# Weight blocks seven to fifteen of a three-layer kernel: ScalarE's first steps wait for the attention rows of chunks zero and one

## The chip, the cores and the metric

One NeuronCore of a Trainium2 chip runs the whole program. The metric is the device time of one execution in microseconds, the median of three runs. Each profile is one execution, taken by the hardware profiler.

## What is computed

Three layers follow one another on 3072 tokens (4 sequences of 768 positions) of width 384.

```
# layer 1: linear attention with the delta rule, one 48 x 48 state per batch and head, 8 heads
y[t]  = q[t] @ state
state = state + beta[t] * outer(k_n[t], v[t] - k_n[t] @ state)     # t = 0 .. 767
# layer 2: x = y as (3072, 384);  384 -> 2048 -> 384
h = x @ w_in
x = (h * sigmoid(1.702 * h)) @ w_out
# layer 3: four experts, 384 -> 1024 -> 384, all of them on every token
out = sum over e of  p[:, e] * (relu(x @ w1[e]) @ w2[e])           # p: normed domain_probs
```

The weights of layer 2 arrive as 64-bit floats; everything else is 32-bit.

## The kernel before

**Attention.** The 768 positions are cut into 12 chunks of 64 positions. Chunk u of all 4 sequences gives 256 rows for layer 2, and two chunks make a tile of 512 rows; there are six tiles. A chunk is a chain that mostly alternates between TensorE and the engines that read its result: keys against the state (L867), a subtraction on VectorE (L874), a first solve (L881), copies to SBUF on ScalarE and VectorE (L184, tile `su`), a cross term (L896), L874 again, a second solve (L881), copies again, the output y (L912 and L913, in two halves), and the state update (L936, added by L953 on VectorE). The inverse that the solves use is made per tile. For tile 0 VectorE makes it. For all later tiles VectorE transposes the Gram matrix (L637), computes norms and rates in small operations (L399 to L425), and GpSimd then runs a chain of 30 elimination steps (L649, then L658 and L660 in turn, then L665); VectorE transposes the result back (L685). The chain of a chunk can't start before that.

**Rows for layer 2.** Chunks 0 and 1 write their rows straight into the operand of layer 2: `take_x` on ScalarE or VectorE (L184, tile `xs`) takes the rounded part, `take_rest` (L930) on VectorE the rest. These tasks are `direct[0]` and `direct[1]`. Later chunks copy y into `stage`, move a fourth of it by DMA (L1049), and are split into `xs` from there (L184 and L1083).

**Layer 2 and its weights.** The weights are 16 blocks f. For each block, layer1 (L1089) makes 128 hidden rows from `xs`, the gate (L1211 and L1213 on ScalarE, L1214 on VectorE) makes `gh`, and layer2_1 (L1196) adds the result into `px`. Each is nine matmuls. Tiles 0 and 1 are halved: blocks 0 to 7 run on the first chunk's 256 columns, then on the second chunk's, and only blocks 8 to 15 on all 512 columns. A block's weights are prepared once. `queue_w1` loads it by SyncE (L222, into `rw`, or into `raw` for blocks 0 and 15), converts the 64-bit floats by two steps on ScalarE (`small` at L293, `low` at L296) and one on VectorE (`shift`, L300), and splits it into two 32-bit parts (`hi`, L305 on ScalarE, and `lo`, L308 on VectorE, which ends as `wdone[f]`). There are six `rw` buffers, so the load of block f waits for `wdone[f - 6]`.

**Layer 3** runs after all tiles of layer 2, in L1089, L1323 and L1353.

**What sets the order.** Nothing is reordered on the chip: each engine runs its queue in order. The queues are written by a planner inside the kernel (`Order` and `Task`, L28 to L148). Every step is a task with an engine, an estimated cost, the tasks it depends on and a priority (lower first). The planner keeps a virtual clock per engine and issues the best task that is ready. Between two matmuls of layer 2 it looks again (`tick`), so attention matmuls are woven into layer 2's. When layer 2 needs something that isn't done yet, `until` issues other tasks until it is. A dependency in the task list orders the plan; the waits on the chip come from the data. A step with another dependency therefore moves on its engine, and by the virtual clocks what stands behind it on all engines can move as well.

Weight steps have priorities of 6 (blocks 0 and 1), 16 (2 to 7) and 33 (8 to 15); chunks 0 and 1 have 0 to 10, and `take_x` has -2. An engine that is free takes what is ready, whatever its priority.

Of the kernel before, what the change touches and what calls it, by code (L numbers as in the profile page):

```python
# [27 lines left out]
class Order:  # L28
# [14 lines left out]
    def task(self, fn, eng, cost, deps=(), lat=0.15, prio=0, slack=0.5, can=None, extra=0.4):  # L43
        t = Task(self, fn, eng, cost, [d for d in deps if d is not None], lat, prio, slack, can, extra)
        return t
# [106 lines left out]
def delta_attention_moe_moe_kernel(  # L152
# [27 lines left out]
    task, tick, until = od.task, od.tick, od.until  # L180
# [40 lines left out]
    def bulk(dst, src):  # L221
        nc.sync.dma_start(out=dst, in_=src)  # L222
# [31 lines left out]
    W, wdone, begun, turns, ended, marks = {}, {}, {}, {}, {}, []  # L254
# [3 lines left out]
    def queue_w1(f, after):  # L258

        kw = dict(prio=(FIRST_W if f < 2 else EARLY_W if f < N_EARLY else LATE_W) + f / 50, slack=0.5)
        later = {F1 - 1: (wdone.get(0),)}
        cell = {}

        def room():
            cell["raw"] = wp.tile([128, 1536], F32, name="rw", tag=f"w{RAW + (f - 1) % 6}")  # L270

        def touch():
            room()
            V.memset(cell["raw"][:, 0:1], 0.0)

        def load():
            if f in (0, F1 - 1):
                t = raw.rearrange("p h c -> p (h c)")
            else:
                if "raw" not in cell:  # L280
                    room()
                t = cell["raw"]
            dst = t.bitcast(I32) if wide else t
            bulk(dst if wide else dst[:, 0:768], w[f])
            if wide:
                pairs = dst.rearrange("p (n t) -> p n t", t=2)
                cell["lo"], cell["hi"] = pairs[:, :, 0], pairs[:, :, 1]
                cell["t"], cell["top"] = cell["lo"].bitcast(F32), cell["hi"].bitcast(F32)
            else:
                cell["t"] = t[:, 0:768]  # L290

        def small():
            nc.scalar.activation(out=cell["top"], in_=cell["top"], func=AF.Prelu, scale=2.0 ** -112, alpha=-2.0 ** 32)  # L293

        def low():
            nc.scalar.activation(out=cell["lo"].bitcast(U32), in_=cell["lo"].bitcast(U32), func=AF.Copy, scale=2.0 ** -29 * (1 - 2.0 ** -16),  # L296
                                 bias=7.5 * 2.0 ** -16 - 0.5)

        def shift():
            nc.vector.scalar_tensor_tensor(out=cell["lo"], in0=cell["hi"], scalar=3, in1=cell["lo"],  # L300
                                           op0=ALU.logical_shift_left, op1=ALU.bitwise_or)

        def hi():
            W[f] = wp.tile([128, 2, 768], F32R, name="w", tag=f"w{RING[f]}")
            nc.scalar.copy(out=W[f][:, 0, :], in_=cell["t"])  # L305

        def lo():
            nc.vector.tensor_tensor(out=W[f][:, 1, :], in0=cell["t"], in1=W[f][:, 0, :].bitcast(F32), op=ALU.subtract)  # L308

        if 6 < f < F1 - 1:  # L310
            after = (*after, wdone[f - 6])
        if 1 < f < 7:
            after = (*after, task(touch, "DVE", 0.07, (marks[f - 2],), prio=1.4))
        dep = task(load, "HW", 2.0 if wide else 1.0, (*later.get(f, ()), *after), lat=1.5, prio=50)
        if wide:
            a = task(small, "ACT", 0.83, (dep,), **kw)
            b = task(low, "ACT", 0.9, (dep, begun[0]), **kw)
            dep = task(shift, "DVE", 0.88, (a, b), **kw)
        h = task(hi, "ACT", 0.73, (dep, wdone.get(f - 1)), **kw)
        wdone[f] = task(lo, "DVE", 0.95, (h,), **kw)  # L320
# [47 lines left out]
    direct = {}  # L368
# [725 lines left out]
    with tc.manual_schedule():  # L1094
# [44 lines left out]
        for f in range(F1):  # L1139
            queue_w1(f, placed[3])  # L1140
# [326 lines left out]
```

## Time and profile before

| | us |
|---|---|
| median of three runs | 1367.26 (1365.63 to 1661.65) |
| the profiled execution | 1365.22 |
| its span, first to last instruction | 1363.3 |
| TensorE busy in the span | 1332.3 |
| VectorE, ScalarE, GpSimd busy | 612.2, 423.1, 221.3 |

The span is the part of the execution that the rows below can explain; 1.9 us lie around it. A busy TensorE is one that had a matmul in flight: a wait that falls between two matmuls that overlap is not seen as idle.

### The profile page before, as it was taken

How to read it: one execution, taken by the hardware profiler on the slowest of the kernel's cores; microseconds unless marked ns; L12 is line 12 of the kernel's file. 1: busy time of each engine (PE TensorE's matmuls, PEld its weight loads, DVE VectorE, ACT ScalarE, POOL GpSimd, SP SyncE). 2: the span in 40 equal slices, each digit the busy share in tenths (PEclk: the TensorE clock that was granted, in tenths of full speed). 3: DMA queues.
4: the chain of work that ended last, by engine and by line, in shares of the span. 5: the costliest groups of instructions: out<-in, count | busy, mean ns of one | idle time of the engine just before them, and what ended most of it. 6: DMA issues, size and time to landing. Idle time of an engine off the chain costs nothing.

```text
span 1363.3 us, 28151 instructions
## 1 busy us (share of the span) xinstructions
PE 1332.3 (98%) x12376; PEld 1118.1 (82%) x12376; DVE 612.2 (45%) x1049; ACT 423.1 (31%) x790; POOL 221.3 (16%) x408
## 2 busy tenths in 40 slices
PE   5899999999999999999999999999999999999998
PEld 4788898778787888788888888888888888888888
DVE  7888584663735224223333234433343333233443
ACT  6873442432424334312222122222222221112111
POOL 4295748055181000000000000000000000000000
PEclk9999999999999999999999999999999999999999
DMA  7640412220201013000010000010010000011111
GB/s 238 217 132 14 113 29 76 63 64 2 74 17 40 5 76 124 8 9 31 31 42 20 1 20 31 32 38 14 0 31 31 32 20 8 0 31 31 32 31 47
DMA packets 36411, 63.30 MB, mean 46 GB/s; under 512 B 18688, under 2 KB 20160, under 8 KB 36288
## 3 DMA queue, kind: packets, MB, share of 16 engines
q1 hardware_dynamic: 36288, 61.50, 14.9%
q8 instruction: 97, 1.59, 0.5%
q14 instruction: 26, 0.21, 0.1%
HBM read 52.58 MB, written 7.91 MB: 44 GB/s over the span
## 4 chain that ended last, share of the span: by engine, by line
PE 92%; DVE 4%; DMA 1%; ACT 1%; issue 1%; SPq 0%; DVEq 0%; ACTq 0%
PE ph L1089 43%; PE po L1323 24%; PE px L1196 14%; PE po L1353 5%; PE y L913 2%; PE ch L881 1%; PE ch L867 1%; PE gp L491 1%; PE ch L896 1%; PE ch L936 1%; DMA rw<-in_w_dram 1%; DVE scr L581 1%; PE gp L554 1%; DVE scr L685 0%; DVE scr L184 0%
## 5 line engine op out<-in xcount | busy, mean ns | idle before, releaser
L1089 PE MATMUL ph<-xs,w 128*128 128x512 f32 (+1 forms) x2736 | 651.3, 380 | 1.7 <-ACT x L184 0.8
L1089 PEld LDWEIGHTS ph<-xs,w 128*128 128x128 f32 x2736 | 494.2, 188 | 96.8 <-ACT x L184 1.2
L1384 DVE SCALAR_TENSOR_TENSOR hh<-ph,hh 128x512 fp32r<-128x512 f32 x192 | 132.5, 690 | 503.4 <-ACT hh L1383 503.4
L1323 PE MATMUL po<-hh,w 128*128 128x512 f32 x1440 | 352.4, 389 | 0.0
L1323 PEld LDWEIGHTS po<-hh,w 128*128 128x128 f32 x1440 | 270.4, 188 | 56.0
L1383 ACT ACTIVATE hh<-ph 128x512 fp32r<-128x512 f32 x192 | 114.8, 598 | 616.7 <-PE ph L1089 616.7
L1196 PE MATMUL px<-gh,w 128*128 128x512 f32 (+1 forms) x1008 | 228.7, 364 | 1.0 <-DVE gh L1214 0.8
L1196 PEld LDWEIGHTS px<-gh,w 128*128 128x128 f32 x1008 | 170.7, 188 | 31.6 <-DVE gh L1214 2.1
L1214 DVE TENSOR_TENSOR gh<-ph,gh 128x512 fp32r<-128x512 f32 (+1 forms) x112 | 68.7, 613 | 149.2 <-ACT gh L1213 148.0
L1211 ACT ACTIVATE ph<-ph 128x512 f32<-128x512 f32 (+1 forms) x112 | 58.4, 521 | 176.0 <-PE ph L1089 164.7
L660 POOL TENSOR_TENSOR scr<-scr,itmp 128x30 f32<-128x30 f32 (+9 forms) x150 | 83.9, 559 | 11.8
L658 POOL TENSOR_TENSOR itmp<-scr 128x30 f32<-128x30 f32 (+9 forms) x150 | 79.5, 530 | 11.2
L1353 PE MATMUL po<-w,hh 128*128 128x384 f32 x384 | 73.9, 342 | 0.0
L1353 PEld LDWEIGHTS po<-w,hh 128*128 128x128 f32 x384 | 69.3, 188 | 2.4
L1213 ACT CAST gh<-ph 128x512 fp32r<-128x512 f32 (+1 forms) x112 | 58.8, 525 | 3.5
L184 ACT COPY su<-ch 64x384 f32<-64x384 f32 (+2 forms) x59 | 27.2, 462 | 63.2 <-PE ch L881 62.5
L1183 DVE TENSOR_TENSOR xs<-x,xs 128x512 fp32r<-128x512 f32 x72 | 45.3, 684 | 0.0
L1182 ACT CAST xs<-x 128x512 fp32r<-128x512 f32 x72 | 39.7, 619 | 0.0
L496 DVE TENSOR_TENSOR pq<-gp,pmask 64x512 f32<-64x512 f32 x48 | 33.1, 689 | 7.0 <-PE gp L491 6.1
L250 DVE TENSOR_TENSOR w<-raw,w 128x768 fp32r<-128x768 f32 x32 | 30.7, 958 | 10.2 <-ACT w L249 9.4
L184 DVE COPY su<-ch 64x384 f32<-64x384 f32 (+2 forms) x45 | 24.2, 537 | 21.3 <-PE ch L881 20.4
L953 DVE TENSOR_TENSOR su<-su,ch 48x384 f32<-48x384 f32 x44 | 24.3, 552 | 20.5 <-PE ch L936 10.3
(133 smaller groups left out, 740.8 us busy)
## 6 DMA issues: line engine op xcount, KB each, us to landing
raw<-in_we_dram SPq DMA_DIRECT2D x32, 384.0 KB, 2.9
rw<-in_w_dram SPq DMA_DIRECT2D x14, 768.0 KB, 4.6
raw<-prd SPq DMA_DIRECT2D x20, 256.0 KB, 3.1
k<-in_k_dram SPq DMA_DIRECT2D x12, 384.0 KB, 4.8
kt<-in_kt_dram SPq DMA_DIRECT2D x24, 192.0 KB, 5.0
pq<-in_q_dram SPq DMA_DIRECT2D x24, 192.0 KB, 3.5
v<-in_v_dram SPq DMA_DIRECT2D x12, 384.0 KB, 3.2
out_dram<-oacc SPq DMA_DIRECT2D x80, 48.0 KB, 1.7
```

Source lines behind the costliest of these rows:

```text
L184: (nc.scalar.copy if e == "ACT" else nc.vector.tensor_copy)(out=out_, in_=in_)
L658: E.tensor_tensor(out=tv, in0=x[:, j:j + 1, j + 1:].broadcast_to([128, m, r]), in1=x[:, 0:m, j:j + 1].broadcast_to([128, m, r]), op=ALU.mult)
L660: E.tensor_tensor(out=x[:, 0:m, j + 1:], in0=x[:, 0:m, j + 1:], in1=tv, op=ALU.add)
L1089: mm(ps, lhsT=w[:, a, kk * 128:(kk + 1) * 128], rhs=xs[kk][:, b, cs], start=kk == 0 and i == 0, stop=kk == KD - 1 and i == 2)
L1196: mm(px[d][:, cs], lhsT=w[:, a, 384 + d * 128:384 + (d + 1) * 128], rhs=gh[:, b, 0:cs.stop - cs.start], start=f == 0 and i == 0 and cs.sta ...
L1211: a = task(lambda: nc.scalar.activation(out=ph, in_=ph, func=AF.Gelu_apprx_sigmoid), "ACT", 0.05 + 0.43 * c, (pe,), **kw)
L1213: a = task(lambda: nc.scalar.copy(out=hi, in_=ph), "ACT", 0.05 + 0.43 * c, (a,), **kw)
L1214: a = task(lambda: nc.vector.tensor_tensor(out=lo, in0=ph, in1=hi.bitcast(F32), op=ALU.subtract), "DVE", 0.07 + 0.53 * c, (a,), **kw)
L1323: mm(po[kk], lhsT=w[:, a, 384 + kk * 128:384 + (kk + 1) * 128], rhs=hh[:, c, :], start=f == 0 and i == 0, stop=f == F2 - 1 and i == 2)
L1353: mm(ps, lhsT=hh[:, a, b * 128:(b + 1) * 128], rhs=w[:, c, 384:768].rearrange("p (k a i) -> p a k i", a=4, k=KD), start=f == 0 and i == 0, ...
L1383: nc.scalar.activation(out=hh[:, 0, :], in_=ph, func=AF.Relu)
L1384: nc.vector.scalar_tensor_tensor(out=hh[:, 1, :], in0=ph, scalar=0.0, in1=hh[:, 0, :].bitcast(F32), op0=ALU.max, op1=ALU.subtract)
```

## The change

`small` of blocks 7 and later depends on `direct[0]` too; for blocks 10 to 15, `small` and `low` both depend on `direct[1]` as well. Nothing that is computed changes. One line is added, so every line behind L316 has a number that is higher by one in the changed kernel.

```
         if wide:
-            a = task(small, "ACT", 0.83, (dep,), **kw)
-            b = task(low, "ACT", 0.9, (dep, begun[0]), **kw)
+            rows = direct[1] if f >= 10 else ()
+            a = task(small, "ACT", 0.83, (dep, *rows, *(direct[0] if f >= 7 else ())), **kw)
+            b = task(low, "ACT", 0.9, (dep, begun[0], *rows), **kw)
             dep = task(shift, "DVE", 0.88, (a, b), **kw)
```

The plan is written anew from there. Three places show it.

The first is ScalarE's queue while chunk 0 gives its rows. `raw_69` holds block 15 here; `rw_337`, `rw_525` and `rw_880` (`rw_881` in the change) hold blocks 2, 3 and 7; `y_849` and `y_890` (`y_888`) are the two halves of chunk 0's output. Before:

```order
L184 COPY stage_73<-su_80 128x12x16
L293 ACTIVATE raw_69<-raw_69 128x768
L305 CAST w_882<-rw_337 128x768
L296 ACTIVATE raw_69<-raw_69 128x768
L184 CAST xs_100<-y_849 128x128
L184 CAST xs_101<-y_849 128x128
L184 CAST xs_102<-y_849 128x128
L305 CAST w_920<-rw_525 128x768
L293 ACTIVATE rw_880<-rw_880 128x768
L184 CAST xs_100<-y_890 128x128
L184 CAST xs_101<-y_890 128x128
L184 CAST xs_102<-y_890 128x128
```

And now:

```order
L184 COPY stage_73<-su_80 128x12x16
L305 CAST w_879<-rw_337 128x768
L184 CAST xs_100<-y_849 128x128
L184 CAST xs_101<-y_849 128x128
L184 CAST xs_102<-y_849 128x128
L296 ACTIVATE rw_881<-rw_881 128x768
L184 CAST xs_100<-y_888 128x128
L184 CAST xs_101<-y_888 128x128
L184 CAST xs_102<-y_888 128x128
L305 CAST w_944<-rw_525 128x768
L184 COPY su_80<-ch0_719 48x8x48
L293 ACTIVATE rw_881<-rw_881 128x768
```

Both steps of block 15 and the first step of block 7 have gone from ahead of the rows; block 7's second step (L296), which waits for the same load, stands ahead of the second half of the rows in their place.

The second place is VectorE's queue from the first gate of layer 2 (`gh`) to the transpose with which the inverse of tile 1 begins (L637, L638 in the change). Before:

```order
L300 SCALAR_TENSOR_TENSOR rw<-rw 128x768
L308 TENSOR_TENSOR w<-rw,w 128x768
L1214 TENSOR_TENSOR gh<-ph,gh 128x256 x2
L637 STREAM_TRANSPOSE scr_98<-scr_97 128x1024
L399 TENSOR_SCALAR sm<-scr_98 128x32
```

And now, the last twelve rows up to the transpose:

```order
L1215 TENSOR_TENSOR gh<-ph,gh 128x256
L184 COPY su<-ch_739 48x8x48
L1215 TENSOR_TENSOR gh<-ph,gh 128x256
L308 TENSOR_TENSOR w<-rw,w 128x768
L300 SCALAR_TENSOR_TENSOR rw<-rw 128x768
L1215 TENSOR_TENSOR gh<-ph,gh 128x256
L308 TENSOR_TENSOR w<-rw,w 128x768
L1215 TENSOR_TENSOR gh<-ph,gh 128x256
L300 SCALAR_TENSOR_TENSOR rw<-rw 128x768
L308 TENSOR_TENSOR w<-rw,w 128x768
L1215 TENSOR_TENSOR gh<-ph,gh 128x256
L638 STREAM_TRANSPOSE scr_98<-scr_97 128x1024
```

The transpose stood behind the gates of blocks 0 and 1; it stands behind those of blocks 0 to 4 now.

The third place is ScalarE's queue at the end of tile 0, where chunk 3's chain runs (`ch_2487` before, `ch_2553` now are a bank of it) and tile 1's operand is split from `stage`. Before:

```order
L1211 ACTIVATE ph<-ph 128x512
L1213 CAST gh<-ph 128x512
L184 COPY su<-ch_2487 64x8x48 x2
L1211 ACTIVATE ph<-ph 128x512
L1213 CAST gh<-ph 128x512
L184 COPY su<-ch_2487 64x8x48 x2
L184 CAST xs<-stage 128x256 x2
L1211 ACTIVATE ph<-ph 128x512
L1213 CAST gh<-ph 128x512
L184 COPY stage<-y 48x2x256 x2
L1211 ACTIVATE ph<-ph 128x256
```

And now:

```order
L1212 ACTIVATE ph<-ph 128x512
L1214 CAST gh<-ph 128x512
L184 COPY su<-ch_2553 64x8x48 x4
L184 CAST xs<-stage 128x256 x2
L184 COPY stage<-y 48x2x256 x2
L1212 ACTIVATE ph<-ph 128x256
```

Three gates of 512-column blocks lay within and around chunk 3's chain; one does now, ahead of both copies, so chunk 3's steps follow each other with little of layer 2 between them.

## Rows read from the trace of the kernel before

**Rows 1.** Busy time of each engine by stretch: start:end, length, then the engines.
```profile
0.00:52.60 52.60, 30.03 (x1144) 27.10 (x1144) 43.60 (x100) 36.02 (x70) 16.83 (x38) 1.00 0.72 231
52.60:120.80 68.20, 66.45 (x1261) 60.05 (x1261) 59.10 (x105) 47.08 (x93) 49.66 (x70) 1.00 0.38 116
120.80:155.50 34.70, 34.70 (x827) 27.24 (x827) 21.21 (x52) 13.53 (x28) 18.98 (x39) 1.00 0.23 63
155.50:1357.70 1202.20, 1199.53 (x9138) 1002.41 (x9137) 486.08 (x790) 326.52 (x600) 135.80 (x262) 1.00 0.11 33
```
**Rows 2.** ScalarE in order of time: start, us, instruction, [idle before and releaser].
```profile
46.95 0.95 ACT L293 ACTIVATE raw<-raw 128x768 f32<-128x768 f32 x1 [0.57 <-DMA raw<-in_w_dram]
...
49.40 0.61 ACT L184 CAST xs<-y 128x128 fp32r<-128x128 f32 x3
...
51.49 0.93 ACT L293 ACTIVATE rw<-rw 128x768 f32<-128x768 f32 x1 [0.69 <-DMA rw<-in_w_dram]
52.30 0.61 ACT L184 CAST xs<-y 128x128 fp32r<-128x128 f32 x3
```
**Rows 3.** SyncE's issues in order of time, the loads of blocks 7 to 9.
```profile
47.15 6.26 SPq L222 DMA_DIRECT2D rw<-in_w_dram  x3
```
**Rows 4.** TensorE in order of time: chunk 0's end, then chunks 2 and 3.
```profile
50.37 1.64 PE L936 MATMUL ch<-su,k 64*48 64x48 f32 x64
52.62 0.38 PE L1089 MATMUL ph<-xs,w 128*128 128x256 f32 x1 [0.61 <-ACT xs L184]
...
55.53 1.39 PE L769 MATMUL gp<-scr,scr 32*32 32x16 f32 x128
...
120.82 1.15 PE L867 MATMUL ch<-su,kt 48*64 48x48 f32 x64
...
136.46 1.10 PE L913 MATMUL y<-pq,su 128*48 128x64 f32 x32
...
143.10 0.88 PE L881 MATMUL ch<-v,scr 32*32 32x48 f32 x64
...
155.53 1.24 PE L1089 MATMUL ph<-xs,w 128*128 128x256 f32 x9
```
**Rows 5.** The chain that ended last, in order of time: one 512-column block's layer 1.
```profile
112.71 2.07 PE ph L1089 x9
```
**Rows 6.** VectorE in order of time: tile 1's inverse, two weight shifts, chunk 3's steps.
```profile
57.68 2.18 DVE L637 STREAM_TRANSPOSE scr<-scr 128x1024 f32<-128x1024 f32 x1
...
91.79 2.76 DVE L300 SCALAR_TENSOR_TENSOR rw<-rw 128x768 int32<-128x768 int32 x2
...
118.70 2.22 DVE L685 STREAM_TRANSPOSE scr<-scr 128x1024 f32<-128x1024 f32 x1 [0.49 <-POOL scr L665]
...
140.80 1.70 DVE L874 TENSOR_TENSOR v<-v,ch 128x384 f32<-128x384 f32 x3
...
144.08 1.14 DVE L184 COPY su<-ch 64x384 f32<-64x384 f32 x2 [1.58 <-PE ch L881]
...
151.20 1.22 DVE L1083 TENSOR_TENSOR xs<-stage,xs 128x256 fp32r<-128x256 f32 x3
```
**Rows 7.** GpSimd in order of time: tile 1's elimination chain.
```profile
64.17 4.27 POOL L649 TENSOR_TENSOR scr<-scr,bt 128x256 f32<-128x256 f32 x4 [11.94 <-DVE bt L425]
...
90.44 0.62 POOL L658 TENSOR_TENSOR itmp<-scr 128x240 f32<-128x240 f32 x1
91.13 1.30 POOL L660 TENSOR_TENSOR scr<-scr,itmp 128x240 f32<-128x240 f32 x1
...
116.32 2.34 POOL L665 TENSOR_TENSOR scr<-scr,bt 128x256 f32<-128x256 f32 x4
```
**Rows 8.** L913 alone in two stretches: length, TensorE, its loads, granted clock, DMA.
```profile
45.00:50.30 5.30, 4.98 (x48) 4.35 (x48) 1.00 0.84 292
78.60:80.20 1.60, 1.42 (x24) 1.34 (x24) 1.00 0.75 273
```
**Rows 9.** SyncE in order of time: chunk 2's rows moved within `stage`.
```profile
139.34 4.73 SPq L1049 DMA_DIRECT2D stage<-scr  x6
```

## The prediction

> **What bounds the kernel now.** I read busy time by stretch first. Up to 52.6 us TensorE is busy for 30.0 us; from there to 1357.7 us it waits for 1.75 us in the first stretch, not at all in the second and for 2.67 us in the long third [rows 1]. So the time is the moment at which layer 2 starts, plus a TensorE queue that hardly waits. The matmuls are the same in the changed kernel. It can gain only before 52.6 us or out of those 1.75 and 2.67 us, and it loses whatever wait it makes.
>
> Next I read the queues in order of time. ScalarE stands at 46.95 us for block 15's load. The first half of chunk 0's rows is cast at 49.40. The second half is cast at 52.30, although its y matmuls ended at 50.37 when L936 began: block 7's first step, at 51.49, stood ahead of it and waited for its load [rows 2, 4]. TensorE's first L1089 then begins at 52.62, after 0.61 us of waiting for those casts [rows 4].
>
> Further on, two waits are hidden with little to spare. Tile 1's inverse begins with L637 at 57.68 us, GpSimd gets its input at 64.17 and ends at 118.66, and L685 ends at 120.92; the first matmul of chunk 2, L867, stands in TensorE's queue at 120.82 [rows 4, 6, 7]. TensorE and the inverse arrive together. Chunk 2's last y, at 136.46, ends at 137.56, its rows are moved in `stage` from 139.34 and split by 152.42, and tile 1's first block begins at 155.53 [rows 4, 6, 9]. Three us are left there.
>
> **The change, part by part.** *First rows.* The change takes away from ahead of them block 15's 0.57 us of waiting and two steps of 0.95 us or so, and block 7's first step (0.93 us after 0.69 us of waiting) [rows 2]. The first half of the rows could be cast some 1.5 us earlier. But block 7's second step isn't tied to chunk 0's rows. The plan puts it ahead of the second half, and it needs the same load, issued at 47.15 behind `wdone[1]`, which nothing here makes earlier; the load was there at 51.49 [rows 2, 3]. So that step runs from 51.49 and the second half of the rows is again cast at 52.30. Layer 1 needs both halves. I cost the headline edit at nothing: 0.
>
> *State update.* Its second half (32 of the 64 matmuls that took 1.64 us [rows 4]) is now behind block 0's and 1's layer 1. Before, it ran while TensorE had to wait anyway. It costs 0.85 us, of which half comes back because block 0's gate has that time to finish: +0.4.
>
> *Up to chunk 2.* More matmuls of layer 2 stand between chunk 1's steps, and later weight steps no longer stand before gates. At most the 1.75 us of waiting go [rows 1]; I walked the queues with durations of the trace and find TensorE ahead by about 1.4 there. With the line above that is -1.0, with -2 and +1 as bounds: all waits gone, or none and the update's 0.85 us in full.
>
> *Loads.* Blocks 11 and 12 are now loaded ahead of chunk 2's q and chunk 4's keys, and the load of block 12 waits for `wdone[6]`. Those inputs are issued later, but are first used by matmuls that stand behind all of chunk 1's chain. That hides it: 0; with that cover gone it would be a load's latency, 4.3 us (47.15 to 51.49).
>
> *Tile 1's inverse.* L637 moves behind the gates of blocks 2 to 4. TensorE reaches the end of block 4's layer 1 at about 64.3: the first two blocks' L1089 to 55.5 as before, half an update 0.85, six half-width groups of nine at half of 2.07, and 1.39 for L769 [rows 4, 5]. With 1.5 us for the gate, an estimate for its two steps on ScalarE and one on VectorE, L637 begins near 65.8 instead of 57.68. To its last small operation it took 6.4 us [rows 6, 7]; now another gate, L783 and two L874 stand among them, some 2 us. GpSimd starts at 74.4, 10 us later. Its chain took 54.5 us [rows 7]. One step of it takes 0.62 us, the next one 1.30 us while VectorE runs L300 [rows 6, 7]: 0.6 us per weight operation beside it. There were 18 such (7 L300, 11 L308) in that time; there are 15 behind the new start, so the chain takes 54.5 - 1.8 = 52.7 us. It ends at 127.1, and L685 (2.22 us) at 129.4. TensorE comes to L867 after layer-2 work worth 33 more 512-column matmuls, 33 x 0.23 = 7.6 us [rows 5], at 128.4 less the 1.0 gained: 127.4. It waits 2.0 us. Bounds: 0 if the chain is faster by that, 4 if L637's start slips as far again.
>
> On that step the row says that a GpSimd operation beside L300 grows by 0.6 us [rows 7]. [...]
>
> *End of tile 0.* Chunk 2's chain shifts as a whole, so its last y now leaves only 18 of layer 2's 512-column matmuls (9 in 2.07 us [rows 5]) to set beside chunk 3's chain: 7 ahead of L867, then 8, 3, 0 and 0 between its steps. From that y to tile 1's first block TensorE has 4.1 us of layer 2 and, from [rows 4], 1.15 (L867), three times 0.88 (L881 twice, L896 alike), 1.10 (y) and about as much for L936: 10.1 us. The chain takes 7 matmuls (1.6), L867 1.15, L874 1.70, L881 0.88, copies 1.14, L896 0.88, L874 for two thirds (1.1), L881 0.88, copies 1.14, y 1.10, L936 1.10 [rows 4, 6], and 0.3 for each of four handovers: 13.9 us. TensorE waits the difference, 3.8 us, in pieces of 0.7 to 1.4. Chunk 2's rows took 14.9 us from that y to the split operand (137.56 to 152.42), because the split stood behind chunk 3's last copies; there it stands again, so it is ready by the chain's end. Before, there was no wait, since 50 matmuls lay where 18 lie now. Bounds: 0, were VectorE and ScalarE free at each step and twice as quick, and 5.
>
> *Sum.* 0 - 1.0 + 2.0 + 3.8 = +4.8 on the profiled execution's 1365.22 us (1363.3 of span and 1.9 around it): 1370.0. That execution is 2.0 under the median of the three runs and 0.4 under the lowest; I state 1370.5. From the bounds, 1363.2 to 1375.2. That is within 2% (27 us), about what a measurement of this kernel can tell from no change.
>
> **The rivals.** *A: the rows do come early, and the rest is covered.* If block 7's load lands by 50.4, the second half's casts follow y at once, 1.9 us before 52.30; with the waits of the first stretch gone and the later ones hidden the time is 1365.2 - 1.9 = 1363.3, not slower than before. For it speaks that the waits at 46.95 and 51.49 are real; against it, that the load is issued at 47.15 in both, and the move of L637.
>
> *B: the inverse becomes the bound.* L637's start slips further, or the chain gains nothing from fewer weight operations: L867 waits 4 us or more, and with the tile's end 1375 us come out. It decides once GpSimd ends after 129.
>
> [...]
>
> [...]
>
> **How the numbers follow.** Forecast 0.63, A 0.18, B 0.10, C 0.09. The forecast's own range is 1366 to 1375; with A and most of C it is 1363.5 to 1377.5. Faster by over 2% has 0.01: the start is too short to give 27 us. Slower has 0.02, from C's far end. The rest, 0.97, is within.
>
> **What would show it.** Right: the second half's casts at 52.3, ahead of them L296 at the end of a wait for a load; L637 near 66; GpSimd's L649 near 74.5; TensorE waiting for L685 at L867 near 127 to 129; gaps in TensorE between chunk 3's steps, 3 to 5 us in all, before tile 1's first block. Wrong: a first L1089 at 51 or before, GpSimd's start under 70, no idle time in TensorE from 120 to 165, or new waits in tiles 2 to 5, where I expect those of before.

## The result, and the profile after

| | before | after | ratio (95% interval) |
|---|---|---|---|
| median, us | 1366.54 | 1377.55 | 1.0092 (1.0063 to 1.0121) |
| lowest of six executions | 1364.54 | 1374.96 | |
| profiled execution, its span | 1365.22, 1363.3 | 1381.48, 1379.8 | |

The change costs 11 us, 0.9%. Forecast were 1370.5 (1363.5 to 1377.5): the right direction, and less than half of the size.

The six executions of the changed kernel spread over 9.6 us, and they go with TensorE's mean granted clock: 1374.96 us at 1.000, 1375.77 at 0.999, 1376.24 at 0.998, 1381.48 at 0.997, 1378.85 at 0.996 and 1384.52 at 0.992. So a part of the loss is clock. It isn't all of it: at a clock of 1.000 there are still 8.4 us.

The busy time by stretch, cut at the same places as in [rows 1] (first layer 1, chunk 2's first matmul, tile 1's first block, layer 3's end):

```profile
0.00:55.45 55.45, 29.83 (x1112) 26.58 (x1113) 42.57 (x98) 33.69 (x67) 16.89 (x38) 1.00 0.70 212
55.45:140.68 85.23, 79.03 (x1327) 69.77 (x1327) 67.31 (x126) 51.25 (x99) 49.98 (x74) 0.96 0.29 97
140.68:170.19 29.51, 27.63 (x795) 21.50 (x794) 16.36 (x31) 11.10 (x24) 24.67 (x48) 1.00 0.24 67
170.19:1374.20 1204.01, 1200.47 (x9147) 1003.10 (x9140) 478.44 (x777) 334.19 (x616) 132.74 (x257) 1.00 0.12 34
```

Length less TensorE's busy time is what it stood idle: 25.62, 6.20, 1.88 and 3.54 us, against 22.57, 1.75, 0 and 2.67 before [rows 1]. That is 10.25 us more idle time. The rest of the span's 16.5 us is busy time: TensorE has the same matmuls and is busy 6.25 us longer with them (1336.96 against 1330.71). About half of that is the clock, by an estimate: in the second stretch the granted clock is 0.96, and 0.04 of 85.23 us is 3.4 us. The other half is not assigned. In the first stretch a reading of 1.00 says nothing ahead of 50 us (before) and 54 us (after), where the trace's clock record begins; four L912 took 0.48 us there at 45 us and 0.34 from 78 us on.

Of the idle time, 3.05 us lie ahead of layer 1. The first solve began 2.9 us late there, behind instructions that stand in the same order in both kernels; from it to layer 1 it is 15.3 us in both. The rows of TensorE, in order of time, before and then after:

```profile
19.51 0.26 PE L563 MATMUL gp<-kt 48*32 48x32 f32 x2 [2.63 <-issue]
...
24.91 2.27 PE L491 MATMUL gp<-pq,kt 48*64 48x64 f32 x61 [2.80 <-issue]
...
35.54 1.04 PE L778 MATMUL gp<-scr,scr 32*32 32x16 f32 x61 [2.10 <-issue]
37.30 1.50 PE L881 MATMUL ch<-v,scr 32*32 32x48 f32 x64 [0.72 <-issue]
```

```profile
40.19 1.50 PE L882 MATMUL ch<-v,scr 32*32 32x48 f32 x64 [0.71 <-issue]
```

TensorE's waits in the second stretch (engine, line and releaser: us in total, times, longest):

```profile
PE px L1197 <- DVE gh L1215: 2.3, 4, 0.7
PE px L1197 <- issue: 2.3, 1, 2.3
...
PE gp L779 <- issue: 0.5, 1, 0.5
```

"Issue" means that the profile shows nothing for which TensorE waited. Before there was no such wait from the first rows to chunk 2; ahead of layer 1 the kernel before has three of 2.1 to 2.8 us, as the rows above show. Both new ones stand in this piece of TensorE's queue, in order of time:

```profile
66.00 0.72 PE L770 MATMUL gp<-scr,scr 32*32 32x16 f32 x64
66.65 0.74 PE L1090 MATMUL ph<-xs,w 128*128 128x256 f32 x4
67.32 0.73 PE L770 MATMUL gp<-scr,scr 32*32 32x16 f32 x64
...
68.89 0.37 PE L779 MATMUL gp<-scr,scr 32*32 32x16 f32 x22
69.78 0.53 PE L779 MATMUL gp<-scr,scr 32*32 32x16 f32 x42 [0.52 <-issue]
70.24 0.85 PE L1197 MATMUL px<-gh,w 128*128 128x256 f32 x5
71.03 0.73 PE L779 MATMUL gp<-scr,scr 32*32 32x16 f32 x64
71.68 0.39 PE L1197 MATMUL px<-gh,w 128*128 128x256 f32 x1
71.90 1.23 PE L1090 MATMUL ph<-xs,w 128*128 128x256 f32 x9
72.97 1.00 PE L1197 MATMUL px<-gh,w 128*128 128x256 f32 x7
76.25 0.28 PE L1197 MATMUL px<-gh,w 128*128 128x256 f32 x1 [2.27 <-issue]
76.46 1.14 PE L868 MATMUL ch<-su,kt 48*64 48x48 f32 x32
...
79.25 1.95 PE L868 MATMUL ch<-su,kt 48*64 48x48 f32 x32
```

Chunk 1's 128 small L770, which stood alone at 55.53 [rows 4], are now in one heap with 128 equally small L779. Then count from the first pause to the second: 42 + 5 + 64 + 1 + 9 + 7 = 128 matmuls, and as many weight loads, 256 instructions. From 60 to 80 us the queue q8, which carries instructions, moved this (packets, MB, share of the DMA engines):

```profile
q8 instruction: 3, 0.05, 1.0%
```

That is 16 KB a packet. In the whole execution q8 moved 97 packets (1.59 MB), and TensorE ran 12376 matmuls and as many weight loads:

```profile
PE 1338.2 (97%) x12376; PEld 1121.9 (81%) x12376; DVE 606.6 (44%) x1033; ACT 430.2 (31%) x804; POOL 224.3 (16%) x416
...
q8 instruction: 97, 1.59, 0.5%
```

That makes 255 of them a packet. So the author's estimate is that one packet brings TensorE's next 256 instructions, and that the two pauses stand one packet apart; no view names the instructions in a packet.

The last L868 in the piece shows the second half of the loss: the same 32 matmuls take 1.95 us instead of 1.14. Behind the pause the clock has fallen (stretch, length, engines, then granted clock, DMA share, GB/s):

```profile
70.00:75.00 5.00, 3.98 (x123) 3.70 (x112) 3.40 (x7) 0.94 (x3) 0.00 (x0) 1.00 0.92 297
75.00:80.00 5.00, 3.75 (x55) 3.26 (x56) 1.06 (x4) 0.00 (x0) 0.00 (x0) 0.79 0.06 17
80.00:85.00 5.00, 5.00 (x83) 4.39 (x83) 2.79 (x12) 1.67 (x4) 0.47 (x1) 0.53 0.01 3
```

From 77.88 to 84.71 us alone the granted clock reads 0.50. In the first of these rows the loads of three weight blocks, chunk 2's q and chunk 4's keys fill the DMA engines (0.92); in the others there is almost no load left.

The other lines that answer to [rows 2], [rows 4], [rows 6] and [rows 7], one engine after the other:

```profile
54.36 0.89 ACT L296 ACTIVATE rw<-rw 128x768 uint32<-128x768 uint32 x1 [2.06 <-DMA rw<-in_w_dram]
55.15 0.41 ACT L184 CAST xs<-y 128x128 fp32r<-128x128 f32 x2
...
69.78 2.01 DVE L638 STREAM_TRANSPOSE scr<-scr 128x1024 f32<-128x1024 f32 x1
...
77.70 0.55 DVE L875 TENSOR_TENSOR v<-v,ch 128x384 f32<-128x384 f32 x1 [3.29 <-PE ch L868]
...
81.31 0.55 DVE L875 TENSOR_TENSOR v<-v,ch 128x384 f32<-128x384 f32 x1 [2.49 <-PE ch L868]
...
84.53 3.51 POOL L650 TENSOR_TENSOR scr<-scr,bt 128x256 f32<-128x256 f32 x4 [29.51 <-DVE bt L426]
...
134.44 2.39 POOL L666 TENSOR_TENSOR scr<-scr,bt 128x256 f32<-128x256 f32 x4
...
138.55 2.24 DVE L686 STREAM_TRANSPOSE scr<-scr 128x1024 f32<-128x1024 f32 x1
```

ScalarE again waits for block 7's load ahead of the second half's casts, only with L296 in L293's place. VectorE's two L875 wait for TensorE's late L868, with tile 1's inverse queued behind them, so GpSimd starts at 84.53 (before 64.17). In the changed kernel layer 2 begins about 3 us later, and chunk 2 (L868 at 140.68) 20 us later. In between, layer 2's matmuls that stood behind L868 were done first, 7.6 us of them by the prediction's count.

### The profile page after: what moved, and what is told of

It reads as the page before. It is cut to its first block, busy times and chain, and to the rows that moved or that the text cites. A ratio compares the mean times of both kernels' runs of the same rounds, so it can differ in the third digit from the quotient of the medians.

```text
span 1379.8 us, 28198 instructions
## 1 busy us (share of the span) xinstructions
PE 1338.2 (97%) x12376; PEld 1121.9 (81%) x12376; DVE 606.6 (44%) x1033; ACT 430.2 (31%) x804; POOL 224.3 (16%) x416
## 3 DMA queue, kind: packets, MB, share of 16 engines
q1 hardware_dynamic: 36288, 61.50, 14.9%
q8 instruction: 97, 1.59, 0.5%
## 4 chain that ended last, share of the span: by engine, by line
PE 77%; POOL 6%; DVE 2%; issue 2%; DMA 0%; ACT 0%; SPq 0%; DVEq 0%; POOLq 0%
PE ph L1090 36%; PE po L1324 24%; PE px L1197 8%; PE po L1354 5%; POOL scr L661 2%; POOL itmp L659 2%; PE y L914 1%; PE ch L882 1%; DVE scr L582 1%; PE ch L937 1%; PE ch L897 0%; POOL scr L650 0%; PE ch L868 0%; DMA pq<-in_q_dram 0%; DVE gh L1215 0%
## 5 line engine op out<-in xcount | busy, mean ns | idle before, releaser
L1090 PE MATMUL ph<-xs,w 128*128 128x512 f32 (+1 forms) x2736 | 652.0, 380 | 2.0 <-ACT xs L184 0.9
L1090 PEld LDWEIGHTS ph<-xs,w 128*128 128x128 f32 x2736 | 495.7, 188 | 97.7 <-ACT x L184 1.2
L1197 PE MATMUL px<-gh,w 128*128 128x512 f32 (+1 forms) x1008 | 231.3, 366 | 6.7 <-DVE gh L1215 4.4
L1197 PEld LDWEIGHTS px<-gh,w 128*128 128x128 f32 x1008 | 171.9, 190 | 36.2 <-DVE gh L1215 6.6
L184 ACT COPY su<-ch 64x384 f32<-64x384 f32 (+2 forms) x66 | 30.6, 464 | 47.9 <-PE ch L882 47.0
L875 DVE TENSOR_TENSOR v<-v,ch 128x384 f32<-128x384 f32 (+1 forms) x56 | 30.0, 550 | 26.2 <-PE ch L868 7.7
L829 POOL TENSOR_TENSOR v<-v,nr 128x192 f32<-128x192 f32 x40 | 20.5, 545 | 105.8 <-DMA v<-in_v_dram 87.1
```

Of the source, the lines that this page charges most:

```text
L1090: mm(ps, lhsT=w[:, a, kk * 128:(kk + 1) * 128], rhs=xs[kk][:, b, cs], start=kk == 0 and i == 0, stop=kk == KD - 1 and i == 2)
L1197: mm(px[d][:, cs], lhsT=w[:, a, 384 + d * 128:384 + (d + 1) * 128], rhs=gh[:, b, 0:cs.stop - cs.start], start=f == 0 and i == 0 and cs.sta ...
```

## The experiments

All ratios are to runs of the kernel before on the same chip. The expectations compare with the first profile of before and after.

| run | median, us | ratio (95% interval) |
|---|---|---|
| e1 the change again | 1382.47 | 1.0111 (1.0089 to 1.0132) |
| e2 loads of blocks 11, 12 back | 1381.54 | 1.0109 (1.0096 to 1.0122) |
| e3 first step of blocks 7 to 14 | 1365.83 | 0.9995 (0.9987 to 1.0004) |
| e4 chunk 1's part | 1380.83 | 1.0105 (1.0090 to 1.0120) |
| e5 update ahead of layer 1 | 1372.81 | 1.0053 (1.0040 to 1.0065) |
| e6 chunk 0's part | 1371.80 | 1.0038 (1.0025 to 1.0050) |
| e7 loads late | 1375.58 | 1.0071 (1.0058 to 1.0084) |
| e8 second steps too | 1369.00 | 1.0020 (1.0009 to 1.0031) |
| e9 all but block 15 | 1367.78 | 1.0011 (1.0002 to 1.0020) |
| e10 block 15 alone | 1380.98 | 1.0106 (1.0091 to 1.0121) |
| e11 block 7, both steps | 1370.04 | 1.0029 (1.0018 to 1.0040) |
| e12 e9 with second steps | 1370.16 | 1.0034 (1.0021 to 1.0047) |
| e13 before, L769 held back | 1380.22 | 1.0098 (1.0083 to 1.0114) |
| e14 the change, L770 early | 1376.20 | 1.0063 (1.0049 to 1.0076) |

**Is it the same in a second profile?** e1 is the changed kernel itself.

> The changed kernel, as it is, with a second profile. If the 2.9 us by which the first solve began late (L882 at 44.71 against 41.81 before) are start-up jitter of one execution, this profile has it near 42 and everything up to layer 1's first L1090 near 52.6 again; if they belong to the changed program, it is near 44.7 again. If the pause of TensorE ahead of chunk 1's first L868 (2.27 us with no releaser, at 73.97) and the granted clock of 0.53 to 0.79 behind it belong to the program, the pause is there again between 70 and 76 and the clock falls behind it; if they are chance, they are gone and the time is near 1375. Either way the time against the kernel before is expected at +8 to +12 us.

The pauses are there again, 0.64 us ahead of the same L779 and 2.00 ahead of the same L1197, and the clock is 0.71 in 75 to 80 and 0.50 in 80 to 85. They belong to the program. The time was expected 8 to 12 us above the kernel before and is 16 above. The first solve was late again (40.47), but in e2, whose queues are the same up to there, it came at 37.57: the start varies from execution to execution.

**Are the reordered loads to blame?** e2 puts the loads of blocks 11 and 12 back behind chunk 2's q and chunk 4's keys:

```
-  dep = task(load, "HW", ..., prio=50)
+  dep = task(load, "HW", ..., prio=50, can=(lambda: placed[4][0].done if 4 in placed else None) if f in (11, 12) else None)
```

> The changed kernel with one thing put back: blocks 11 and 12 are loaded behind chunk 2's q and chunk 4's keys, as before; the order of every computing instruction stays. Theory L (the three loads of 2.3 MB in a row from 63 to 69 us and the q and keys behind them make TensorE pause at 74 and the clock fall): the pause and the low clock are gone, the state products L868 of chunk 1 start some 2 to 3 us earlier and take 1.1 us each, and the time falls by 2.5 to 6 us, to 1372 to 1375. Theory I (the loss is the inverse that starts late and the end of tile 0): the time stays within 1.5 us of the changed kernel's run beside it, whatever the pause does.

Theory L fell: the time is that of e1. The pause didn't go, it grew at the first of the two places, in L779, where the DMA engines were still 0.64 busy:

```profile
70.59 0.53 PE L779 MATMUL gp<-scr,scr 32*32 32x16 f32 x42 [3.23 <-issue]
```

**Which part of the change?** e3 and e4 take the two parts apart, e9 and e10 split the blocks.

```
e3   a: (dep, *(direct[0] if 7 <= f < 15 else ()))        b: (dep, begun[0])
e4   a: (dep, *rows)    b: (dep, begun[0], *rows)          rows = direct[1] if f >= 10 else ()
e9   as the change, with f < 15 in both conditions
e10  a: (dep, *rows)    b: (dep, begun[0], *rows)          rows = direct[1] if f == 15 else ()
```

> Of the change only this: the first step (L293) of blocks 7 to 14 waits for the first chunk's rows; block 15 and the second-chunk part stay as before. The orders of all engines are nearly those of before, with L637 ahead of block 2's gate. Theory 1 (block 7's second step, which isn't tied to the rows, waits for the same load, so the headline edit is worth nothing): second-half casts at 52.3 as before, time within 1 us of before. Rival A (the rows come early): casts at 50.4 and the time 1.9 us less, 1364.5. A loss over 3 us here would say that the first part itself costs.

> Of the change only this: both steps of blocks 10 and later wait for the second chunk's rows; blocks 7 to 9 as before. In this order the inverse's L637 stands behind two more gates than before, and blocks 11 and one more are loaded in a pair ahead of chunk 2's q. Theory I (late inverse and end of tile 0): L638 near 62 to 66, chunk 2's first L868 5 to 9 us later than before, and +4 to +8 us in all. Theory L (pause and clock from loads): only two loads stand in a row, so the pause is under 1 us and the clock holds; +1 to +4 us.

> The change for blocks 7 to 14; block 15 as before, its steps free of the rows. In this order TensorE, GpSimd and the loads stand nearly as before; on ScalarE the first steps of blocks 7 to 14 and the second ones of 10 to 14 are behind the rows. Theory B (block 15's two steps, which filled ScalarE's wait for chunk 0's rows and made the plan hold layer 1 until both halves of the state update were in, are what displaces the rest): within 2 us of before, 1364 to 1368. Rival P (the later weight steps of blocks 10 to 14 make gates and weights late): 1370 or more, with TensorE waiting for L308 or L1215 between 60 and 120.

> The complement: only block 15's two steps wait for the second chunk's rows, as in the change; blocks 7 to 14 as before. Theory B: the second half of L937 stands behind layer 1 of blocks 0 and 1, L770 and L638 slip (L638 near 66 to 68, GpSimd's L650 near 80), TensorE pauses without a releaser in 65 to 77, the clock falls, and the time is 1372 to 1382. Rival P: under 1369.

The headline of the change, first steps behind chunk 0's rows, is worth nothing for blocks 7 to 14, and the reason is in e3's ScalarE rows: L296 takes the place and waits for the same load.

```profile
51.98 0.92 ACT L296 ACTIVATE rw<-rw 128x768 uint32<-128x768 uint32 x1 [0.70 <-DMA rw<-in_w_dram]
52.79 0.42 ACT L184 CAST xs<-y 128x128 fp32r<-128x128 f32 x2
```

The complement pair names the block: all but 15 costs 0.1%, block 15 alone 1.1%, as much as the whole change. So the later weight steps of the other blocks are not the cause. In e4 the loss was forecast at 4 to 8 us and is 14; theory L's "pause under 1 us" was 2.3 us.

**Why block 15?** Before, its two steps fill ScalarE's wait for chunk 0's rows. Without them the plan has the rows' split done earlier by its virtual clock, and starts layer 1 when only half of the state update has been issued. The other half (priority 0.9) then takes the turn of chunk 1's L770 (10.5), and L770, the transpose L638 behind it and GpSimd slip. This way through the plan is read from the task list and the queues. e5 keeps the update ahead of layer 1, e6 has the update inside layer 1 but L770 in its old place, e13 makes the slip alone in the kernel before, and e14 takes the slip out of the changed kernel:

```
e5   writes.append(wr)                                     # the state updates' tasks
-        until(*split)
+        until(*split, *writes[:2])
e6   rows = ()                                             # chunk 0's part alone, block 15 included
e13  -   can=None if gn.start else ...
     +   can=None if gn.start else (lambda: 59.3) if u == 1 else ...
e14  -   prio=p, can=None if gn.start else ...
     +   prio=0.5 if u == 1 else p, can=None if gn.start else (lambda: 52.0) if u == 1 else ...
```

> The changed kernel with one thing put back: both halves of chunk 0's state update (L937) stand ahead of layer 1, as before. In this order chunk 1's L770 stands again right behind block 1's layer 1 and L638 ahead of block 2's gate. Theory D (the update's second half, now inside layer 1, takes the place in the plan that L770 had; L770 and all of tile 1's inverse slip by four gates, TensorE's small matmuls come in one heap, it pauses there, and the clock falls): L638 near 58, GpSimd's L650 near 64.5, no pause without a releaser behind 55 us, clock 1.00 throughout, time 1364 to 1368. Rival W (the loss comes from the weight steps that now stand behind the rows, so that gates and weights are late): 1372 or more.

> Of the change only the first line's part: the first step of blocks 7 to 15 waits for chunk 0's rows; nothing waits for chunk 1's. In this order the second half of the state update stands behind layer 1 of blocks 0 and 1, as in the changed kernel, but L770 and L638 keep the places they had before. Theory D: it is the slip of L770 and the inverse that costs, so 1365 to 1368. Theory U (the update inside layer 1 itself is what starts the low clock, with the 0.9 to 1.2 us wait ahead of the first L1090): clock under 1.00 in 50 to 60, and 1369 to 1375.

> The kernel before, with none of the change; only chunk 1's L769 (in the changed kernel L770) is held back, and comes behind block 3's layer 2, as far back as in the changed kernel. Tile 1's inverse slips with it, and 256 small matmuls (L769, L778) stand within 18 of layer 1's and 2's. Block 15's steps and both halves of the state update stay where they were. Theory S (the slip is what costs): L637 near 66, a pause of TensorE without a releaser of 2 us or more in 63 to 77, the clock under 1.00 behind it, time 1373 to 1380. Rival G (block 15's displaced steps cost on ScalarE, whatever L770 does): under 1369.

> The changed kernel with chunk 1's L770 put ahead of the state update's second half, right behind block 1's layer 1; the inverse stands as early as before, everything else is the change. Theory S: L638 near 58 to 60, GpSimd's L650 near 65, no pause of 2 us in 60 to 77, time within 0.4% of before, 1366 to 1371. Rival G: 1373 or more.

e13 is the clearest: with nothing of the change in it, the slip (and the plan written anew behind it) makes 1.0098. Its TensorE rows show the same heap and the same pause, and behind it a clock of 0.68 and 0.50:

```profile
63.78 0.73 PE L769 MATMUL gp<-scr,scr 32*32 32x16 f32 x64
65.11 0.73 PE L769 MATMUL gp<-scr,scr 32*32 32x16 f32 x64
...
70.10 0.56 PE L778 MATMUL gp<-scr,scr 32*32 32x16 f32 x45 [2.72 <-issue]
71.38 0.82 PE L778 MATMUL gp<-scr,scr 32*32 32x16 f32 x64
73.71 1.95 PE L867 MATMUL ch<-su,kt 48*64 48x48 f32 x32
```

```profile
70.00:75.00 5.00, 4.90 (x144) 4.48 (x145) 0.99 (x4) 0.90 (x1) 0.00 (x0) 0.68 0.09 24
75.00:80.00 5.00, 5.00 (x69) 4.34 (x67) 2.01 (x8) 2.21 (x5) 0.00 (x0) 0.50 0.00 0
```

But the slip isn't the only way there. In e14 L638 is back at 59.50 and the time is still 1.0063 (theory S said 1.004 at most, and the wait of over 2 us that it excluded is there); e5 recovers only half as well. Both times lie where the rivals put them (G: 1373 or more, W: 1372 or more), though G failed in e13 and W's late steps cost 0.1% in e9. Both have this in their place (e14, then e5):

```profile
71.74 1.65 PE L1090 MATMUL ph<-xs,w 128*128 128x256 f32 x7 [3.31 <-DVE w L308]
```

```profile
68.42 1.10 PE L1090 MATMUL ph<-xs,w 128*128 128x256 f32 x7 [1.34 <-DVE w L308]
```

The profile puts these waits down to block 4's L308. In e14 it had ended at 68.34, three us early, and 1497 matmuls of the program stand ahead of this L1090, as many as ahead of the changed kernel's second pause. The same holds in e5, where L308 ended at 68.37 and late instructions can't be told from it, and in e6, where the same L1090 waits 0.87 us with no releaser. So the author's reading is that e14's wait is more likely one for late instructions too. An instruction packet started 3.06 us ahead of it (68.68), and in e5 2.96 us ahead (65.46). That reading is from counting and from the packets' times, not from an experiment. In e5 and e14 the clock falls behind it (e14: 0.64 in 70 to 75, 0.50 in 75 to 80; e5: 0.51 and 0.50). e6 holds its clock at 1.00 in its profile, which is the fastest of its five executions; its 0.4% is as much as theory U wanted, without U's sign. It also has the update inside layer 1 with no slip of L770, so the one doesn't by itself bring the other.

**Do the weight loads make the pause?** e7 leaves the computing queues as they are up to there and loads blocks 10 to 12 only after chunk 1's rows:

```
+  dep = task(load, ..., can=(lambda: hdone[1, 0].done if (1, 0) in hdone else None) if f in (10, 11, 12) else None)
```

> The changed kernel with blocks 10, 11 and 12 loaded only after chunk 1's rows; all computing engines' orders up to there stay. Theory F (TensorE's pauses near 66 to 76 are its next instructions coming late beside 2.3 MB of weight loads; each 16 KB packet of q8 covers 128 matmuls with their weight loads): pauses under 1 us in all, clock 1.00 in 70 to 85, chunk 1's second L868 done by 77, and the time falls to 1371 to 1375 although these blocks' weights come later. Rival (the heap of small matmuls outruns its instructions whatever the loads do): a pause of 2 us or more at the same instructions, clock down to 0.5 to 0.8, time as the changed kernel's, 1376 to 1382.

Theory F held at its place, and its time came out at the upper edge (1375.58). TensorE's pauses, the granted clock there, and where the loads went (two kinds of rows, each in order of time):

```profile
67.33 0.53 PE L779 MATMUL gp<-scr,scr 32*32 32x16 f32 x42 [0.62 <-issue]
...
92.41 0.46 PE L492 MATMUL gp<-pq,kt 48*64 48x64 f32 x16 [1.49 <-issue]
101.02 1.11 PE L1090 MATMUL ph<-xs,w 128*128 128x256 f32 x8 [1.04 <-issue]
```

```profile
70.00:75.00 5.00, 5.00 (x87) 4.63 (x86) 2.06 (x8) 0.74 (x2) 0.00 (x0) 1.00 0.02 3
75.00:80.00 5.00, 4.24 (x142) 3.35 (x142) 4.50 (x15) 3.45 (x7) 1.75 (x2) 1.00 0.02 5
...
85.00:90.00 5.00, 4.86 (x123) 4.23 (x122) 4.54 (x13) 2.98 (x8) 4.29 (x10) 1.00 1.02 420
```

With the DMA engines idle (0.03 from 65 to 70 us, then 0.02) the heap of small matmuls runs with one pause of 0.62 us, the clock stays at 1.00, chunk 1's L868 start at 71.57 and 73.78, and GpSimd at 78.25. Two new pauses come where the loads now are and just behind them. The ratio falls from e1's 1.0111 to 1.0071; the change's first result, 1.0092, is too wide to tell from it.

The instruction packets' own times in the traces say where the loads come in. Up to the L779 of the first pause, count 128 matmuls back. In e7 the packet started 0.87 us behind that one, and TensorE went on 2.74 us behind the packet, 3.6 in all; the 128 matmuls took 3.0. In e2, e4, e10 and e13 the packet started 2.85 to 3.47 us behind that matmul, and TensorE went on 2.4 to 2.9 us behind the packet. In the first profile of the change it started 0.89 us behind at that place and 4.02 us behind at the next, ahead of the long pause. So beside the loads the packet starts later; from there on it takes no longer.

**Could the rows come early after all?** Rival A wanted that. e8, e11 and e12 make block 7's second step wait too:

```
e8   rows = direct[1] if f >= 10 else direct[0] if f >= 7 else ()         # both steps
e11  rows = direct[0] if f == 7 else ()                                   # both steps, of block 7 alone
e12  rows = direct[1] if 10 <= f < 15 else direct[0] if 7 <= f < 10 else ()
```

> The second steps (L296) of blocks 7 to 9 wait for chunk 0's rows too, and both steps of blocks 10 and later for chunk 1's, as in the change. Theory 1 (only the second step kept the second half's casts at 52.3): the casts follow the last y at once, at 50.5, and the first L1090 begins 1 to 1.8 us earlier than before; L638 stands ahead of block 1's gate, so nothing slips, and the time is 1363 to 1366. Rival: block 7's weights come later by a step and TensorE waits for them, or L868 of chunk 2 for the inverse: 1367 or more.

> Only both steps of blocks 7 to 9 wait, for chunk 0's rows; the rest as before (the first step alone did nothing). Theory 1: the second half's casts follow the last y at once; first L1090 begins 13.1 to 13.9 us behind the first solve L882 (14.9 before) and the time is 1363 to 1365.5. Rival: the gain is given back, because block 7's weights or tile 1's inverse are later: 1366 to 1369.

> The change without block 15, with the second steps of blocks 7 to 9 waiting for chunk 0's rows as well. Theory 1 and theory B together: first L1090 begins 13.1 to 13.9 us behind the first L882, nothing slips, 1362.5 to 1365.5, the best of all. Rival P: the later weight steps of blocks 10 to 14 cost more than the rows gain, 1367 or more.

In e11 ScalarE's casts do follow, at 50.69 (before 52.30), and layer 1's first matmul starts 14.4 us behind the first solve. Before it was 15.3 (37.30 to 52.62), not the 14.9 that two expectations name:

```profile
51.88 0.39 PE L1090 MATMUL ph<-xs,w 128*128 128x256 f32 x1
53.32 2.30 PE L1090 MATMUL ph<-xs,w 128*128 128x256 f32 x17 [1.05 <-DVE xs L931]
```

The next 17 wait for VectorE's part of the rows and start 15.9 us behind the first solve, before 16.0. In e11 the gain ends on VectorE. In e8 the two numbers are 13.6, as hoped, and 14.9; in e12 14.8 and 15.5. Still all three are slower, e8 and e12 where their rivals have them and e11 above its rival's range. The best is 1.0020; none beats the kernel before, and no kernel of this study does.

## Why the prediction was right or wrong

By stretch, the profiled execution loses 2.85, 17.03, -5.19 and 1.81 us. With the 7.6 us of layer 2 that moved from the third stretch to the second this is 2.9, 9.4, 2.4 and 1.8; forecast were 0, -1.0, 2.0 + 3.8 and 0. The direction was right, but in part by luck: the terms that made the forecast slower measured 2.4 instead of 5.8, and the loss is in the stretch that was to gain.

**First rows, 0: right**, shown by e3 and by the L296 rows. Rival A's mechanism (e11) is real on ScalarE, and VectorE's L931 takes it back there.

**Loads, 0: right for their order** (e2 against e1), but the sentence "with that cover gone it would be a load's latency" looked at the wrong customer. With three loads moved the pause ahead of L779 is 0.62 us, and q8's packet starts 0.87 us behind the matmul 128 ahead of it (e7) instead of 2.85 to 3.47 (e2, e4, e10, e13); that the loads delay TensorE's own instructions is the author's reading of it.

**State update, +0.4, and up to chunk 2, -1.0 with it: the step that failed.** The state update's term priced the half as work, 0.85 us with half of it covered. It put at nothing that chunk 1's L770 slips as well: what moves isn't only L637's start but 128 small matmuls, which then meet 128 others beside the heaviest loads. The slip is 0.98% or 13.4 us (e13), where the prediction's sum has 4.8 for everything.

The premise under -1.0, that a TensorE queue with the same matmuls loses only its waits for other engines, left out two things that are no dependency: the pauses without a releaser (0.52 and 2.27 us), and the clock (0.79 and 0.53 behind them). In place of -1.0 the profiled execution has 9.4 us. The stretch's idle time rose by 4.45 us, 2.8 of them the two pauses, and the low clock took 3.4.

**Tile 1's inverse, +2.0: chain right, consequence wrong.** The sums inside it are slightly off (the terms for 64.3 add up to 64.0, those for 74.4 to 74.2). No row gives its 1.5 us for the gate; block 4's three steps took 1.22 us (68.64 to 69.86). GpSimd's chain took 52.3 us (84.53 to 136.83); 52.7 were forecast, by the row on GpSimd beside L300. Its start was forecast at 74.4 and was 84.53. Some 3 us of that are the later start of layer 2, most of the rest VectorE's two waits for L868 (3.29 and 2.49). TensorE showed no wait for L686 at L868, and it can't have one: L868 makes `ch` from `su` and `kt`, and the inverse (`scr`) is first read by the solve. The plan has L868 behind the inverse, the chip doesn't hold it back. In e10 it ran while L686 did (VectorE, then TensorE):

```profile
140.71 2.21 DVE L686 STREAM_TRANSPOSE scr<-scr 128x1024 f32<-128x1024 f32 x1 [2.32 <-POOL scr L666]
```

```profile
141.27 1.15 PE L868 MATMUL ch<-su,kt 48*64 48x48 f32 x64
```

Before, too, L867 began at 120.82, ahead of L685's end at 120.92 [rows 4, 6].

**End of tile 0, +3.8: right in kind, too large.** Chunk 3's chain shows gaps of 0.17, 0.70, 0.20, 0.57 and 0.18, together 1.8 us; the stretch has 1.88 of idle time. No row gives the 0.3 us for a handover; these gaps are what the run shows in its place. The matmuls beside the chain are as forecast: 7, 8, 3, 0 and 0.

**The rivals.** B's deciding point was passed (GpSimd ended after 129) without B's wait. C, that TensorE's clock falls in the gaps of chunk 3's chain, had 0.09, and the clock did fall. The larger fall, to 0.79 and 0.53, is in another place, behind the pause of 2.27 us at 74. At C's own place the clock holds at 1.00 in the first profile. In e1, the same kernel with the same gaps (0.17, 0.71, 0.20, 0.57 and 0.18), it fell to 0.77 in 170 to 175, and the 30 L914 there took 1.68 us instead of 1.09; in e10 it fell to 0.81 and 0.51 in 165 to 175. So C's place costs too, in some executions: by the clock 1.7 us in e1 (0.77 and 0.89 of five us each), 3.4 in e10. The prediction's upper end of 1377.5 and its 0.02 for slower take in a larger loss at C's place, which no run shows; 1.7 and 3.4 us stand in its place. The slow y matmuls at 45 us [rows 8] lie ahead of the trace's clock record, so their 1.00 is no reading.

**What stays open.** The pause and the clock always came together in the larger losses, so their shares are known only from single profiles. What fills the 8.4 us of the execution at a clock of 1.000 is not shown, since it left no profile. About half of the loss stays when the slip is taken out (e5, e14). The 0.2 to 0.4% of e6, e8, e11 and e12 were not taken apart. e14's long wait is assigned by a count and a packet's time, as said.

## What to carry to other kernels

Before moving a step that "only fills a wait", ask what its place does to the plan: here two idle-time steps held the start of a layer until a half chunk's update was in, and without them 128 small matmuls met 128 others. Small matmuls get through their instructions fast (128 with their loads in 3.0 us in e7), and the pauses stood where two heaps of them met bulk loads (0.74 and 0.92 of the DMA engines here), so keep them apart from each other and from bulk loads, and look for waits without a releaser and count the instructions between them. Price a pause on TensorE by what the clock does behind it (0.79 and 0.53 over five us each behind 2.27 us here), not by its own length.

## What was not expected of the hardware

TensorE paused 0.5 to 3.2 us without a releaser, ahead of the same L779 (after, e1, e2, e4, e10; in e13 ahead of an L778) and in after and e1 once more 128 matmuls and as many weight loads later. Of the 128 matmuls before each, 118 and 106 were L770 and L779 in the first profile, and the DMA engines were 0.64 to 0.96 busy with loads in these runs; with them idle (0.03, e7) the pause was 0.62 us. By the packets' times in the traces it went on 2.3 to 2.9 us behind an instruction packet in these profiles (67.16 and 69.78, 73.80 and 76.25 in the first).

The clock fell to 0.50 to 0.53 behind the pauses of 2 us and more (after, e1, e10, e13, e14) or to 0.66 (e2, e4), and in e5 to 0.50 behind waits of 1.34 and 0.65. In six profiles it also fell, to 0.66 to 0.79, behind the wait of 1.15 to 1.77 us ahead of layer 1 (e1, e2, e7, e9, e10, e14); in others with such a wait it did not (e4 with 1.87, e5 with 1.20, e6 with 1.83). What decides between them was not tried, nor why the gaps of chunk 3's chain did it in e1 and e10 alone.
